# A retention-and-MLP kernel: the first product of the second-to-last chunk with seven products for eight, its sums by kind

## The chip, the core and the metric

One core of one Trainium2 chip. The metric is the device time of one execution in microseconds (us); a kernel's time is the median of its runs.

## The reference

Retention attention, then a two-layer perceptron with GELU. It is cut here to what is computed, for batch B = 4, heads H = 8, sequence S = 768, head size D = 64:

```python
for t in range(S):
    state = gamma * state + outer(k[t], v[t])      # for each batch and head
    y[t] = scale * q[t] @ state
x = y as (3072 tokens, 512)                        # d_model = 512
h = x @ w_in                                       # d_ff = 2048
out = gelu_tanh(h) @ w_out                         # back to 512
```

## The kernel before, in words

**Chunks and stages.** The sequence is cut into six chunks of 128 steps (c = 0 to 5, `NCk` = 6), each with the four batches, so 512 tokens. A chunk goes through three stages: attention, which leaves its tokens in `xT[c]`; M1, x times `w_in` with the GELU, which leaves g; and M2, g times `w_out`, which leaves the output rows. While PE works on M1 and M2 of chunk c, the attention of chunk n = c + 1 is put between their matmuls, and chunk m = c + 2 is loaded and prepared (`load`, `prep_qk`, `prep1`).

**What sets the order.** The order is written out by hand. `run(units, after)` goes through a list of units, and behind unit i it issues what `after[i]` lists. Each engine takes its own instructions strictly in the order in which the program issues them. In the loop `for c in range(2, NCk)` the 16 units 0 to 15 are M1 and the 14 units 16 to 29 are M2.

**M2 with seven products.** `units_w(c)` computes M2 of 2 x 2 blocks with seven products instead of eight. The table `PROD` lists them as n = 0 to 6: bank (X or Z), left operand, right operand. A block operand is a pair such as (0, 0); an operand that is a sum of blocks is a number, its kind 1 to 4. Each unit is one product n for one half a (eight matmuls, with fp = 0 to 7 in order), so unit 16 is n = 0, a = 0, unit 20 is n = 2, a = 0, and unit 26 is n = 5, a = 0. Product 2 uses the sum of kind 2, product 3 kind 1, product 4 kind 3, and product 5 kind 4. The sums of g are made by `g_sums(eng, c, f0, f1, p0, p1, keys)`: for each kind in `keys` one elementwise instruction of 128 x 512 on POOL or DVE (`tt`, line 387), for the pairs fp = f0 to f1 - 1. Kind 1 is the sum of g blocks (0, 1) and (1, 1), kind 2 is kind 1 minus block (0, 0), kind 3 is (0, 0) minus (0, 1), kind 4 is (1, 0) minus kind 2. `win_sums` and `x_sums` make the like sums of `w_in` and of x, on DVE.

**M1 in two forms.** In chunks 2 to 4, `moe1(c, fc)` computes M1 the plain way: each unit has four matmuls of 512 columns (line 348) and one GELU (line 364). In chunk 5, `units_h(c)` uses seven products: four groups G = 0 to 3, each with seven products of four matmuls with 256 columns (line 571). Its parts are `first` (products 0 and 1), `second` (2 and 3), `third` (4 and 5) and product 6. `keep` copies a bank to SBUF (product 0 on ACT, 2 on DVE, 3 on the engine named in the call), `add` adds such a copy to a bank, on DVE (products 1, 4, 5), and `many((G, n), ...)` issues GELUs on ACT. A product that goes on in a bank (n = 2, 4, 6 in X, n = 5 in Z) waits until the bank's copy or add has read it. The GELU of product 5 gives block (0, 0) of g, of product 4 block (1, 0), of product 1 block (0, 1), of product 6 block (1, 1). Group G covers the pairs fp = 2G and 2G + 1, so `g_sums(..., 4, 6, ...)` needs group 2 and `g_sums(..., 6, 8, ...)` group 3.

**Attention in pieces.** `att_AY(c, bs, tag, ca, abs_, eng)` computes the outputs of chunk c for the batches `bs` (`mm_yc`, `mm_yi`, then `ev_Y` on DVE into `xT`) and the scores of chunk `ca` for the batches `abs_` (`mm_A`, then `ev_A`, DVE's product with the mask into `a_sb`). `att_S` updates the state; for the last chunk there is nothing to update. Scores take two banks of the four with the tag "att"; `units_h` holds one such bank for each group from product 0 to the group's last GELU.

**Slots.** The load tiles q32 and k32 have 8 slots each and v32 has 6; `win_sums`, `x_sums` and the copies of `units_h` use free slots of these for their results.

Of the kernel before, what the change touches and what calls it, by code (L numbers as in the profile page):

```python
# [16 lines left out]
def kernel(  # L17
# [12 lines left out]
    NCk = S // C  # L30
# [3 lines left out]
    NF = d_ff // 128  # L34
# [25 lines left out]
    att = ctx.enter_context(tc.tile_pool(name="att", bufs=4))  # L60
# [79 lines left out]
    def copy_on(eng, out, in_):  # L140
        if eng is nc.scalar:
            eng.copy(out=out, in_=in_)  # L142
        else:
            eng.tensor_copy(out=out, in_=in_)
# [31 lines left out]
    def bank(tag, dt=F32, shape=(128, NHP, 128), name="ps"):  # L176
        return psum.tile(list(shape), dt, tag=tag, bufs=BANKS[tag], name=name)
# [167 lines left out]
    def moe1_mm(c, fc, out, t0, t1):  # L345
        wi, wr = w_in_of[fc]
        for kc in range(NHP):
            nc.tensor.matmul(  # L348
                out=out,
                lhsT=w_in_sb[wi][:, kc, wr * 128:(wr + 1) * 128],  # L350
                rhs=xT[c][:, kc, t0:t1],
                start=(kc == 0),
                stop=(kc == NHP - 1),
                skip_group_check=True,
            )

    def g_tile(c, fc):
        if (c, fc // 8) not in g_sb:
            g_sb[c, fc // 8] = gp.tile([128, 8, B * C], F16, tag=f"g{fc // 8}", name="g")
        r = fc % 8 // 2 * 2  # L360
        return g_sb[c, fc // 8][:, r:r + 2]

    def gelu(out, in_):
        nc.scalar.activation(out=out, in_=in_, func=AF.Gelu_apprx_tanh, scale=1.0)  # L364

    def moe1(c, fc):
        h_ps = bank("h", shape=(128, B * C), name="h_ps")
        moe1_mm(c, fc, h_ps, 0, B * C)
        gelu(g_tile(c, fc)[:, fc % 2], h_ps)
# [16 lines left out]
    def tt(eng, out, in0, in1, op):  # L386
        eng.tensor_tensor(out=out, in0=in0, in1=in1, op=op)  # L387
# [8 lines left out]
    def g_sums(eng, c, f0, f1, p0=0, p1=2, keys=(1, 2, 3, 4)):  # L396
        g = g_sb[c, f0 // 4].rearrange("p (f r) (a b t) -> p r b f a t", r=2, a=2, b=2)
        i = f0 % 4
        q = {
            (r, b): g[:, r, b][:, i:i + f1 - f0, p0:p1] for r in range(2) for b in range(2)  # L400
        }
        t = {j: s_g[j][:, f0:f1, p0:p1] for j in s_g}
        ops = (
            (1, q[0, 1], q[1, 1], ALU.add),
            (2, t[1], q[0, 0], ALU.subtract),
            (3, q[0, 0], q[0, 1], ALU.subtract),
            (4, q[1, 0], t[2], ALU.subtract),
        )
        for j, in0, in1, o in ops:
            if j in keys:  # L410
                tt(eng, t[j], in0, in1, o)
# [33 lines left out]
    def x_blk(c, K, col):  # L445
        x = xT[c].rearrange("p (K k) (a b t) -> p K b k a t", K=2, a=2, b=2)
        return x[:, K, 1 - col]
# [101 lines left out]
    def units_h(c):  # L549
        ps, snap = {}, {}  # L550

        def lhs_h(key, pr, k):
            if key in s_g:
                return t_in[key, pr // 4][:, k, pr % 4]
            K, r = key
            wi, wr = w_in_of[2 * pr + r]
            return w_in_sb[wi][:, 2 * K + k, wr * 128:(wr + 1) * 128]

        def rhs_h(key, k):
            if key in s_g:  # L560
                return s_x[c, (key - 1) // 2][:, (key - 1) % 2, k]
            return x_blk(c, *key)[:, k]

        def mm(G, n):
            k, lk, rk, new, stop = PROD[n]
            if new:
                tag = "att" if k == "X" else "h" if n == 1 else "o"
                ps[G, k] = bank(tag, shape=(128, 2, 2, 128), name="h_ps")
            for p in range(2):
                for kc in range(2):  # L570
                    nc.tensor.matmul(  # L571
                        out=ps[G, k][:, p],
                        lhsT=lhs_h(lk, 2 * G + p, kc),
                        rhs=rhs_h(rk, kc),
                        start=(new and p == 0 and kc == 0),
                        stop=(stop and kc == 1),
                        skip_group_check=True,
                    )

        def keep(eng, G, n):  # L580
            tag = {0: "q32", 2: "k32", 3: "v32"}[n]
            t = ld.tile([128, 2, 2, 128], F32, tag=tag, bufs=6 if n == 3 else 8, name="h_sb")
            copy_on(eng, t, ps[G, PROD[n][0]])
            snap[G, SNAP[n]] = t

        def add(G, n):
            t = snap[G, ADD[n][2]]
            tt(nc.vector, t, ps[G, PROD[n][0]], t, ALU.add)

        def act(G, n):  # L590
            r, col, nm = ADD.get(n, (1, 0, None))
            p0 = 2 * G
            if (c, p0 // 4) not in g_sb:
                g_sb[c, p0 // 4] = gp.tile([128, 8, B * C], F16, tag=f"g{p0 // 4}", name="g")
            g = g_sb[c, p0 // 4].rearrange("p (f r) (a b t) -> p r b f a t", r=2, a=2, b=2)
            gelu(
                g[:, r, 1 - col][:, p0 % 4:p0 % 4 + 2],
                snap[G, nm] if nm else ps[G, "X"],
            )

        V, A = nc.vector, nc.scalar

        def first(G):
            mm(G, 0)
            keep(A, G, 0)
            mm(G, 1)
            add(G, 1)

        def second(G, eng):
            mm(G, 2)  # L610
            keep(V, G, 2)
            mm(G, 3)
            keep(eng, G, 3)

        def third(G):
            mm(G, 4)
            add(G, 4)
            mm(G, 5)
            add(G, 5)

        def many(*what):
            for G, n in what:
                act(G, n)

        return [
            lambda: first(0),
            lambda: first(1),
            lambda: (second(0, A), many((0, 1))),
            lambda: (second(1, V), many((1, 1))),
            lambda: third(0),  # L630
            lambda: (third(1), many((0, 4), (0, 5))),
            lambda: (mm(0, 6), many((0, 6), (1, 4))),
            lambda: first(2),
            lambda: mm(1, 6),
            lambda: (first(3), many((1, 5), (1, 6))),
            lambda: (second(2, A), many((2, 1))),
            lambda: (second(3, V), many((3, 1))),
            lambda: third(2),
            lambda: (third(3), many((2, 4), (2, 5))),
            lambda: (mm(2, 6), many((2, 6), (3, 4))),  # L640
            lambda: (mm(3, 6), many((3, 5), (3, 6))),
        ]

    def units_0():
# [92 lines left out]
    def run(units, after):  # L737
        for i, u in enumerate(units):
            u()
            for f, *args in after.get(i, ()):  # L740
                f(*args)

    VE, AC, PO, SY = nc.vector, nc.scalar, nc.gpsimd, nc.sync
# [172 lines left out]

    for c in range(2, NCk):
        n, m = c + 1, c + 2
        after = {} if n == NCk else {
            12: [(att_AY, n, (), "att", n, (0, 1), None)],  # L920
            19: [(att_AY, n, (0, 1), "h", n, (2, 3), VE)],
            22: [(att_S, n, 0, 1)],
            25: [(att_AY, n, (2, 3), "h", n, (), AC), (att_S, n, 2, 3)],
        }

        def more(at, *what):
            after[at] = after.get(at, []) + list(what)

        for i in range(4 if n < NCk else 0):
            at = 4 * i + 3  # L930
            after[at] = [(g_sums, PO, c, 2 * i, 2 * i + 2)] + after.get(at, [])
        if n == NCk:
            t12, t34 = (1, 2), (3, 4)
            after = {
                7: [(g_sums, PO, c, 0, 2, 0, 2, t12)],
                9: [(g_sums, PO, c, 2, 4, 0, 2, t12), (g_sums, PO, c, 0, 2, 0, 2, t34)],
                15: [(g_sums, VE, c, 4, 6, 0, 2, t12), (g_sums, VE, c, 6, 8, 0, 2, t12)],
                19: [(g_sums, VE, c, i, i + 2, 0, 2, t34) for i in (2, 4, 6)],
            }
        if c in (3, 4):  # L940
            for i in range(2):
                more(i, (win_sums, 2 * (c - 3) + i))
        if c == 4:
            more(27, (x_sums, n))
        if m < NCk:
            more(0, (load, m))
            for b in range(B):
                more((18, 20, 23, 26)[b], (prep_qk, m, b))
                more(24, (prep1, PO, "v", m, b))
        m1 = units_h(c) if n == NCk else [(lambda fc=fc: moe1(c, fc)) for fc in range(NF)]  # L950
        run(m1 + units_w(c), after)


# [28 lines left out]
```

## Time and profile before

| | |
|---|---|
| median of 7 runs | 206.87 us (206.63 to 207.76) |
| profiled execution | 207.08 us |
| its span, first to last instruction | 205.3 us |
| busy: PE, DVE, ACT, POOL | 194.6, 119.6, 104.4, 128.8 us |
| M1 of chunk 4 (plain), on PE | 145.97 to 160.57 us |
| M2 of chunk 4, on PE | 160.57 to 175.70 us |
| M1 of chunk 5 (seven products), on PE | 175.70 to 189.05 us |
| sum of g on POOL, 128 x 512 | 1.153 us each |
| the same sum on DVE | 0.42 us (0.46 with kind 1) |
| GELU of 128 x 512 | 0.60 us from PSUM, 0.63 from SBUF |
| copy or add of a bank on DVE | 0.68 us |

Busy time is the union of an engine's instructions; the chain of waits goes back from the last instruction to what released it, step by step. In lines of the profile, L387 is a line of the kernel, `o_ps<-w_out,g` is output tile and input tiles, x16 a count, and brackets hold the idle time before an instruction and what ended it. PEld is PE's weight load. Times of a stage are taken at the start of PE's first matmul of it.

### The profile page before, as it was taken

To read this page: it belongs to the slowest core of one execution; us is meant where nothing else is said; L and a number is where in the kernel's file an instruction comes from. 1 tells how busy PE (TensorE), PEld (TensorE's weight loads), DVE (VectorE), ACT (ScalarE), POOL (GpSimd) and SP (SyncE) were. 2 spreads that over 40 slices of the span, in tenths; PEclk is the share of its full clock that TensorE was granted. 3 is DMA by queue.
4 is the path that set the end of the run, shared out by engine and by line. 5 is a ranking of instruction groups with operands and counts; after the bars stand their busy time and mean duration, and the time that the engine had idled before them with its cause. 6 is when DMAs were issued, how large, how long until landed. Compare 5 with 4: busy or idle time off the path is not lost.

```text
span 205.3 us, 4729 instructions
## 1 busy us (share of the span) xinstructions
PE 194.6 (95%) x1916; PEld 140.4 (68%) x1916; DVE 119.6 (58%) x271; ACT 104.4 (51%) x186; POOL 128.8 (63%) x130
## 2 busy tenths in 40 slices
PE   5697999999999999999999999999999999998993
PEld 1355746877688888644778644778644788886882
DVE  5256669669970449701379911289902284889730
ACT  2284464463379417566545365635365411588321
POOL 0589333952189999389997269997269980239000
PEclk9999999999999999999999999999999999999999
DMA  6999999999976797999995999842430000400004
GB/s 155 287 263 207 206 206 265 348 317 206 345 175 102 176 241 171 206 286 240 220 208 130 107 337 231 200 102 54 126 129 3 2 0 3 204 3 0 2 22 185
DMA packets 87094, 34.24 MB, mean 167 GB/s; under 512 B 80032, under 2 KB 84512, under 8 KB 87072
## 3 DMA queue, kind: packets, MB, share of 16 engines
q1 hardware_dynamic: 73920, 19.25, 44.3%
q0 software_dynamic: 6624, 12.58, 23.7%
q10 hardware_dynamic: 6528, 2.10, 4.1%
q8 instruction: 15, 0.25, 0.5%
q14 instruction: 7, 0.06, 0.1%
HBM read 27.63 MB, written 6.29 MB: 165 GB/s over the span
## 4 chain that ended last, share of the span: by engine, by line
PE 81%; ACT 5%; DVE 4%; DMA 3%; POOL 3%; SPq 2%; issue 1%; DVEq 0%; ACTq 0%
PE h_ps L348 33%; PE o_ps L490 30%; ACT g L364 4%; DMA k<-in_k_dram 3%; PE o_ps L654 3%; PE y_ps L242 3%; PE a_ps L207 3%; PE o_ps L687 2%; PE y_ps L229 2%; DVE st L285 2%; POOL qk L158 2%; PE s_ps L266 1%; PE h_ps L571 1%; SPq L85 1%; POOL w_in L329 1%; DVE h_sb L387 1%
## 5 line engine op out<-in xcount | busy, mean ns | idle before, releaser
L348 PE MATMUL h_ps<-xT,w_in 128*128 128x512 f16 (+2 forms) x424 | 73.6, 327 | 0.5 <-ACT g L364 0.5
L364 ACT ACTIVATE g<-h_ps 128x512 f16<-128x512 f32 (+1 forms) x86 | 50.3, 588 | 29.1 <-PE h_ps L348 28.9
L348 PEld LDWEIGHTS <-w_in 128*128 128x128 f16 x424 | 39.1, 98 | 30.2 <-issue 1.8
L220 DVE TENSOR_TENSOR a_sb<-a_ps,mask 128x512 f16<-128x512 f32 x48 | 30.1, 683 | 37.8 <-PE a_ps L207 37.7
L387 POOL TENSOR_TENSOR s_g<-g 128x512 f16<-128x512 f16 x35 | 40.3, 1153 | 15.9 <-ACT g L364 15.8
L490 PEld LDWEIGHTS <-s_g 128*128 128x128 f16 x320 | 30.2, 98 | 4.7 <-POOL s_g L387 0.7
L490 PE MATMUL o_ps<-t_w,s_g 128*128 128x256 f16 x240 | 28.1, 273 | 0.0
L490 PEld LDWEIGHTS <-g 128*128 128x128 f16 x240 | 23.4, 98 | 3.9 <-ACT g L364 0.6
L158 POOL TENSOR_TENSOR v<-v,cst 128x512 f16<-128x512 f32 x20 | 20.3, 1041 | 5.9 <-DMA v<-in_v_dram 5.8
L387 POOL TENSOR_TENSOR s_g<-s_g,g 128x512 f16<-128x512 f16 x18 | 20.8, 1153 | 1.4
L285 DVE SCALAR_TENSOR_TENSOR st<-st,cst,s_ps 64x128 f16<-64x128 f16 (+1 forms) x80 | 20.6, 318 | 0.7 <-PE s_ps L266 0.5
L387 POOL TENSOR_TENSOR s_g<-g,s_g 128x512 f16<-128x512 f16 x17 | 19.6, 1154 | 0.0
L490 PE MATMUL o_ps<-w_out,g 128*128 128x256 f16 x160 | 18.5, 273 | 0.3 <-ACT g L364 0.3
L523 POOL DMA_DIRECT2D out_dram<-o_sb x8 | 5.9, 737 | 16.2 <-DVE o_sb L387 15.3
L258 DVE TENSOR_TENSOR xT<-y_ps,dec 128x512 f16<-128x512 f32 x20 | 13.0, 686 | 4.0 <-PE y_ps L242 3.8
L142 ACT CAST qk<-q 128x512 f16<-128x512 f32 x20 | 12.4, 620 | 3.8 <-DMA q<-in_q_dram 3.7
L387 DVE TENSOR_TENSOR o_sb<-o_ps,s_p 128x512 f32<-128x512 f32 (+1 forms) x7 | 4.3, 616 | 15.8 <-ACT qk L142 8.0
L142 ACT CAST qk<-k 128x512 f16<-128x512 f32 x20 | 12.4, 621 | 0.6 <-DMA k<-in_k_dram 0.4
L519 ACT COPY o_sb<-o_ps 128x512 f32<-128x512 f32 (+1 forms) x5 | 2.7, 543 | 18.2 <-PE o_ps L490 17.6
L513 ACT COPY s_u<-o_ps 128x512 f32<-128x512 f32 (+1 forms) x6 | 3.1, 515 | 17.2 <-PE o_ps L490 12.0
L490 PE MATMUL o_ps<-w_out,s_g 128*128 128x256 f16 x80 | 9.6, 273 | 0.0
L490 PE MATMUL o_ps<-t_w,g 128*128 128x256 f16 x80 | 9.5, 273 | 0.0
(77 smaller groups left out, 230.2 us busy)
## 6 DMA issues: line engine op xcount, KB each, us to landing
out_dram<-o_sb POOLq DMA_DIRECT2D x10, 512.0 KB, 4.7
k<-in_k_dram SPq DMA_DIRECT2D x18, 256.0 KB, 4.7
q<-in_q_dram SPq DMA_DIRECT2D x18, 256.0 KB, 4.5
v<-in_v_dram SPq DMA_DIRECT2D x18, 256.0 KB, 5.2
w_in<-in_moe_w_in_dram POOLq DMA_DIRECT2D x4, 512.0 KB, 8.7
w_out<-in_moe_w_out_dram POOLq DMA_DIRECT2D x4, 512.0 KB, 13.8
q<-in_q_dram POOLq DMA_DIRECT2D x4, 256.0 KB, 11.2
k<-in_k_dram POOLq DMA_DIRECT2D x4, 256.0 KB, 9.5
```

The source lines that it names most:

```text
L142: eng.copy(out=out, in_=in_)
L158: eng.tensor_tensor(out=t, in0=src, in1=cst[:, col:col + H].unsqueeze(2).broadcast_to([128, H, Dh]), op=ALU.mult,)
L207: nc.tensor.matmul(out=ps[j][:, hp], lhsT=t[j * 64:(j + 1) * 64, 1, hp], rhs=t[j * 64:(j + 1) * 64, 0, hp], start=True, stop=True,)
L220: nc.vector.tensor_tensor(out=s, in0=ps[j], in1=mask[:, j], op=ALU.mult)
L242: nc.tensor.matmul(out=y_ps[j * 64:(j + 1) * 64, hp], lhsT=h16["v", c, b][:, 2 * hp + j], rhs=a_sb[c, b, j][:, hp], start=(c == 0), stop=True,
L258: nc.vector.tensor_tensor(out=x, in0=ps, in1=dec, op=ALU.mult)
L285: nc.vector.scalar_tensor_tensor(out=t[:, :, hp], in0=t[:, :, hp], scalar=cst[sl, OG + hp:OG + hp + 1], in1=s_ps[sl, :, hp], op0=ALU.mult, ...
L348: nc.tensor.matmul(out=out, lhsT=w_in_sb[wi][:, kc, wr * 128:(wr + 1) * 128], rhs=xT[c][:, kc, t0:t1], start=(kc == 0), stop=(kc == NHP - ...
L364: nc.scalar.activation(out=out, in_=in_, func=AF.Gelu_apprx_tanh, scale=1.0)
L387: eng.tensor_tensor(out=out, in0=in0, in1=in1, op=op)
L490: nc.tensor.matmul(out=po, lhsT=lhs(c, lk, fp, a), rhs=rhs(rk, fp), start=(new and fp == 0 and (last or a == 0)), stop=(stop and fp == NP ...
L654: nc.tensor.matmul(out=ps[k][:, a], lhsT=lhs(0, lk, fp, a), rhs=rhs(rk, fp), start=(first and fp == 0 and a == 0), stop=(stop and fp == NP ...
```

## The change

Five things are changed.

- M1 of chunk 4 is computed by `units_h` too (`seven = c >= NCk - 2`), with the sums it needs: `win_sums` runs in chunks 2 and 3 instead of 3 and 4, and `x_sums` for chunk 4 is issued behind unit 28 of chunk 3, for chunk 5 behind unit 28 of chunk 4 (it was 27).
- In chunk 4 the attention of chunk 5, which stood behind the units 12, 19 and 25, stands behind 17, 21 and 26, all in M2.
- In chunk 4 the sums of g, four kinds at a time behind the units 3, 7, 11 and 15 before, are ordered by kind: kinds 1 and 2 of group 0 behind unit 7, kinds 1 and 2 of group 1 and kind 3 of group 0 behind unit 9, and the other eleven behind unit 15. All are on POOL as before.
- In chunk 5 the sums behind unit 19 are ordered by kind as well (kind 3 of the groups 1 to 3, then kind 4).
- In `units_h`, which both chunks now use, the copy of product 3 in group 3 is made by ACT instead of DVE, and the last GELUs come in the order (3, 5), (3, 4), (2, 6), (3, 6) instead of (2, 6), (3, 4), (3, 5), (3, 6).

```diff
-            lambda: (second(3, V), many((3, 1))),
+            lambda: (second(3, A), many((3, 1))),
             lambda: third(2),
             lambda: (third(3), many((2, 4), (2, 5))),
-            lambda: (mm(2, 6), many((2, 6), (3, 4))),
-            lambda: (mm(3, 6), many((3, 5), (3, 6))),
+            lambda: (mm(2, 6), many((3, 5), (3, 4))),
+            lambda: (mm(3, 6), many((2, 6), (3, 6))),
...
     for c in range(2, NCk):
         n, m = c + 1, c + 2
+        seven = c >= NCk - 2
         after = {} if n == NCk else {
+            17: [(att_AY, n, (), "att", n, (0, 1), None)],
+            21: [(att_AY, n, (0, 1), "h", n, (2, 3), VE)],
+            26: [(att_AY, n, (2, 3), "h", n, (), AC)],
+        } if seven else {
             12: [(att_AY, n, (), "att", n, (0, 1), None)],
             19: [(att_AY, n, (0, 1), "h", n, (2, 3), VE)],
             22: [(att_S, n, 0, 1)],
...
-        for i in range(4 if n < NCk else 0):
-            at = 4 * i + 3
-            after[at] = [(g_sums, PO, c, 2 * i, 2 * i + 2)] + after.get(at, [])
-        if n == NCk:
-            t12, t34 = (1, 2), (3, 4)
-            after = {
-                7: [(g_sums, PO, c, 0, 2, 0, 2, t12)],
-                9: [(g_sums, PO, c, 2, 4, 0, 2, t12), (g_sums, PO, c, 0, 2, 0, 2, t34)],
-                15: [(g_sums, VE, c, 4, 6, 0, 2, t12), (g_sums, VE, c, 6, 8, 0, 2, t12)],
-                19: [(g_sums, VE, c, i, i + 2, 0, 2, t34) for i in (2, 4, 6)],
-            }
-        if c in (3, 4):
+        def sums(eng, keys, *fs):
+            for f in fs:
+                g_sums(eng, c, f, f + 2, 0, 2, keys)
+
+        if not seven:
+            for i in range(4):
+                after[4 * i + 3] = [(g_sums, PO, c, 2 * i, 2 * i + 2)] + after.get(4 * i + 3, [])
+        elif n < NCk:
+            more(7, (sums, PO, (1, 2), 0))
+            more(9, (sums, PO, (1, 2), 2), (sums, PO, (3,), 0))
+            more(15, (sums, PO, (1, 2), 4, 6), (sums, PO, (3,), 2, 4, 6), (sums, PO, (4,), 0, 2, 4, 6))
+        else:
+            more(7, (sums, PO, (1, 2), 0))
+            more(9, (sums, PO, (1, 2), 2), (sums, PO, (3, 4), 0))
+            more(15, (sums, VE, (1, 2), 4, 6))
+            more(19, (sums, VE, (3,), 2, 4, 6), (sums, VE, (4,), 2, 4, 6))
+        if c in (2, 3):
             for i in range(2):
-                more(i, (win_sums, 2 * (c - 3) + i))
-        if c == 4:
-            more(27, (x_sums, n))
+                more(i, (win_sums, 2 * (c - 2) + i))
+        if c >= NCk - 3 and n < NCk:
+            more(28, (x_sums, n))
...
-        m1 = units_h(c) if n == NCk else [(lambda fc=fc: moe1(c, fc)) for fc in range(NF)]
+        m1 = units_h(c) if seven else [(lambda fc=fc: moe1(c, fc)) for fc in range(NF)]
```

## The prediction

> **What bounds the kernel now.** I read the chain of waits first, then the stages, then the two stretches that the change touches, engine by engine. The chain gives TensorE (PE) 81% of the span. From 60 us on it is nearly unbroken PE work, up to the first matrix product (M1) of the last chunk. Stage lengths and busy times, cut where PE changes from M1 to M2 (start:end, length, then busy us of PE, weight load, DVE, ACT, POOL):
>
> ```profile
> 130.09:145.97 15.88, 15.88 (x210) 13.74 (x208) 11.07 (x27) 6.50 (x12) 11.95 (x12) 1.00 0.46 104
> 145.97:160.57 14.60, 14.60 (x83) 6.62 (x81) 5.69 (x13) 9.54 (x16) 11.52 (x11) 1.00 0.18 73
> 160.57:175.70 15.13, 15.13 (x177) 13.16 (x176) 7.87 (x14) 2.35 (x4) 8.49 (x9) 1.00 0.01 2
> 175.70:189.05 13.35, 12.74 (x115) 10.92 (x113) 11.54 (x20) 10.67 (x21) 6.95 (x8) 1.00 0.20 80
> ```
>
> These are M2 of chunk 3, M1 and M2 of chunk 4, M1 of chunk 5. Where all products are eight-fold (second row) PE is the only limit. Where seven products are used (last row), DVE and ACT are busy 11.5 and 10.7 of 13.35 us and PE starts to wait. The chain of waits says the same:
>
> ```profile
> 146.13 11.35 PE h_ps L348 x52
> 157.48 0.55 PE a_ps L207 x16
> 158.03 2.70 PE h_ps L348 x12
> 160.73 3.49 PE o_ps L490 x32
> ...
> 186.69 0.69 DVE h_sb L387
> 187.38 0.02 issue
> 187.40 2.76 ACT g L364 x5
> 190.16 0.05 issue
> 190.21 11.76 PE o_ps L490 x106
> ```
>
> The last five GELUs, behind DVE's adds, hold M2 of chunk 5. PE's timeline has both waits in brackets:
>
> ```profile
> 188.61 0.60 PE L571 MATMUL h_ps<-s_x,w_in 128*128 128x256 f16 x4 [0.60 <-DVE h_sb L387]
> 189.05 0.82 PE L490 MATMUL o_ps<-w_out,g 128*128 128x256 f16 x6
> 190.21 3.01 PE L490 MATMUL o_ps<-w_out,g 128*128 128x256 f16 x26 [0.34 <-ACT g L364]
> ```
>
> POOL, in chunk 4, makes 16 sums without a gap, from 150.37 on:
>
> ```profile
> 150.37 1.14 POOL L387 TENSOR_TENSOR s_g<-g 128x512 f16<-128x512 f16 x1 [2.28 <-ACT g L364]
> ...
> 165.28 1.15 POOL L387 TENSOR_TENSOR s_g<-s_g,g 128x512 f16<-128x512 f16 x1
> 166.40 1.15 POOL L387 TENSOR_TENSOR s_g<-g 128x512 f16<-128x512 f16 x1
> 167.51 1.15 POOL L387 TENSOR_TENSOR s_g<-g,s_g 128x512 f16<-128x512 f16 x1
> ```
>
> 16 sums from 150.37 to 168.66 are 1.143 us each. The one at 165.28 is the last sum of kind 2. It ends at 166.43, and product 2, which started at 165.72, reads it as its seventh operand (fp 6), at 165.72 + 6 x 0.109 = 166.38. So POOL's list is **already level with PE here**, and each operand is waited for alone.
>
> **What the Trainium skill says.** "TensorE: Matmul & The Clock Gate", Back-to-back issue gap: a warm matmul of N columns takes N/2.4 + 2.5 ns, 109 ns at 256; the chain has 32 in 3.49 us, 109. "ScalarE: Activation LUTs", What ACT_TABLE_LOAD costs: 186 ns + 0.833 N, back-to-back ones overlapping by 93, an estimated 520 ns at 512; the trace has GELUs 520 to 537 apart. "GPSIMD Engine Reference", Engine selection: a two-input elementwise operation is about 2x slower than on VectorE; here it is worse, 1.153 us against 0.42 for the same sum. "SBUF — State Buffer", on the shared port pair: a DVE operation with two SBUF inputs and a POOL operation exclude each other. This fits DVE's sum at 189.22, which took 0.92 while POOL worked until 189.86.
>
> **How I replay M1 with seven products.** Each engine works in program order. From the timelines: 4 matmuls 0.437 us, results 0.16 later; a DVE copy or add of PSUM 0.68 long, next start 0.60 later; a GELU 0.62, next 0.53 (from PSUM 0.58, 0.48); an ACT copy 0.585, next 0.47; 0.04 from engine to engine. Gn below is group G, product n. A product that accumulates waits for the copy or add of what its bank holds. The replay of chunk 5 before, against its trace, in us from the stage's start on PE, and of the stages after:
>
> | | trace 5 before | replay 5 before | replay 4 after | replay 5 after |
> |---|---|---|---|---|
> | first add (0,1) | 1.31 | 1.30 | 1.73 | 1.30 |
> | GELU (0,6) ends | 6.96 | 6.95 | 7.15 | 6.95 |
> | product (3,6) starts | 12.91 | 12.91 | 12.68 | 12.48 |
> | M1 ends on PE | 13.35 | 13.34 | 13.11 | 12.91 |
> | GELU (3,5) ends | 14.45 | 14.46 | 13.88 | 13.68 |
> | GELU (2,6) ends | 13.41 | 13.41 | 14.90 | 14.70 |
> | GELU (3,6) ends | 14.94 | 14.95 | 15.38 | 15.18 |
>
> In chunk 4 the first add is 0.43 later, because DVE makes x_sums(4) at 146.23 to 147.7 (the place and length of four of today's win sums); the end is 0.2 later for it.
>
> **Part by part.**
> *Copy (3,3) to ACT.* DVE loses 0.60, so add (3,4), for which product (3,6) waits, comes 0.43 sooner, bounded then by the earlier matmuls. ACT gains 0.47: copy (3,3) at 10.52, GELU (3,1) 10.99, (2,4) 11.52, (2,5) 12.06 (chunk 4).
> *GELU order.* (3,5) goes ahead but waits for add (3,5), which ends at 13.22, while ACT idles 0.6. Then (3,5) 13.26, (3,4) 13.79, (2,6) 14.32, (3,6) 14.80. M2's product 0 needs (3,5) at its seventh matmul and gets it sooner; but (2,6), which the sums of group 2 need, is **1.3 us later** than in the old order.
> *Chunk 5.* M2's seventh matmul starts at max(12.91 + 0.66, 13.68 + 0.06) = 13.74, where today it is at 190.21 - 175.70 = 14.51: **-0.77**. DVE's sums: (2,6) ends 14.70, the four of kinds 1, 2 are done by 16.7, and product 2 wants the last at 17.2; kinds 3, 4 are done by 19.7, product 4 starts at 20.1. Nothing new is late, so the 0.77 lasts to the end. If POOL's six sums (7.05 to 14.2) ran into DVE's, 0.5 would be lost of that.
> *Chunk 4, PE alone.* M1 falls from 14.60 (14.05 of products, 0.55 of attention scores) to 13.11, of which 112 x 0.109 = 12.2 is work. M2 is 15.13 + 0.55 (the scores moved in) plus 0.16 wait for GELU (3,5) and 0.13 for the score banks, which group 3's GELU frees: 15.97 in all, sum 29.0 against 29.73: -0.7.
> *POOL's list in chunk 4.* Still 16 sums, but five in M1 (7.24 to 13.15) and **eleven** (4 of kinds 1 and 2, 3 of kind 3, 4 of kind 4) behind GELU (2,6): 14.99 + 11 x 1.142 = 27.55. On the way the last of kind 2 ends at 19.56; product 2 would read it at 13.11 + 0.16 + 3.49 + 0.69 + 0.66 = 18.1, so PE waits 1.5. Then product 2 ends at 20.70, attention 1.66 to 22.36, product 3 to 24.11, product 4 (kind 3 done at 23.0) to 25.86; product 5 reads the last of kind 4 at 26.5 and gets it at 27.60: 1.1 more. After that come 2 matmuls 0.22, attention 1.11, and 24 matmuls 2.62: 31.55. So chunk 4 takes 31.55 for 29.73: **+1.82**.
> *Attention at 17, 21, 26.* The same instructions. DVE: masks of batches 2, 3 end at 26.1, unit 26 needs them at 27.8; x_sums(5) ends at 32.5, 0.95 into chunk 5, before the first add at 1.3. Cover 0.35; without it M1 of chunk 5 would slip by what exceeds it.
> *Win sums a chunk sooner.* In M1 of chunk 2 DVE has a gap of 10.96 before 96.89; eight sums take 3.0. Nothing. They hold four slots of the load tiles sooner; SP issues chunk 4's loads (88.55 on) behind the transposes of chunk 3, whose casts free the other four. Nothing; a load held past 103 us would delay the casts.
> *POOL's stores* of chunk 4 stand behind the sums but are ready only at about 31: nothing.
>
> **Sum.** +1.82 - 0.77 = +1.05. The profiled execution took 207.08 (span 205.3), within 0.1% of the median 206.87: 206.87 + 1.05 = **207.9**.
>
> **Unknown costs.** PE's waits of 1.5 and 1.1 us are longer than any in its steady part. The Trainium skill ("TensorE: Matmul & The Clock Gate", The HAM clock gate) puts the fall to half clock after some 3.4 us idle, which this trace doesn't show, so I take 0; one such window at half clock would cost an estimated 1.7. A sum on POOL could be 1.11 (its shorter spacing here) to 1.15 long: -0.4 to +0.1. The replay's error was 0.05; with x_sums in front, 0.3 either way.
>
> **Rivals.**
> 1. *Faster, POOL's list is not late.* Then -0.7 - 0.77: 205.4. It decides if the eleven sums end by 25.0, when product 5 would want the last without any wait: 0.91 us a sum, or GELU (2,6) 2.5 us sooner. For it: PE has less work in both chunks. Against: 35 sums of this form at 1153 ns.
> 2. *Chunk 5 gains nothing*, because ACT takes over what DVE sheds (M1 there already has ACT at 10.67 of 13.35): 206.87 + 1.8 = 208.7. Against: (3,5) needs only add (3,5).
> 3. *POOL's list is late, but less*: kind 2 overlaps more, or (2,6) comes 0.5 to 1 us sooner since ACT's small waits shrink: 207.1, no measurable difference.
>
> **Chances.** Forecast 0.62 (207.5 to 208.4), rival 2 and worse 0.12, rival 3 0.14, rival 1 0.12. About 0.3% (0.62 us) can be told from no change: slower 0.74, same 0.14, faster 0.12. The range goes from 206.9, inside rival 3, to 208.7.
>
> **What would show it.** Chunk 4: M1 some 13.1 on PE; waits of PE for s_g on POOL near 2.6 us in all, 0.7 today; POOL idle 1.8 before eleven sums in a row; the last of them some 4 us before chunk 5 starts. Chunk 5: M1 12.9, product (3,6) without most of its 0.60 wait. Wrong: POOL waits under 1 us, or GELU (2,6) before 14.0.

## The result, and the profile after

The kernel after takes 208.16 us (median of 15 runs, 207.66 to 209.29) against 206.96 us (36 runs) for the kernel before: ratio 1.0066, 95% interval 1.0050 to 1.0082. It is **slower by 1.0 to 1.7 us**; the prediction was 207.9, 0.9 to 1.0 above before.

The stages after, cut as before where PE changes from one product to the next (start:end, length, then busy us of PE, weight load, DVE, ACT, POOL): M1 and M2 of chunk 4, M1 of chunk 5, M2 of chunk 5 to the end.

```profile
145.69:158.87 13.18, 12.87 (x115) 10.93 (x113) 12.02 (x22) 10.62 (x20) 7.16 (x7) 1.00 0.20 81
158.87:177.27 18.40, 16.25 (x195) 13.34 (x193) 10.28 (x19) 3.77 (x7) 12.96 (x13) 1.00 0.00 1
177.27:190.33 13.06, 12.75 (x115) 10.93 (x113) 11.03 (x19) 10.64 (x20) 6.60 (x8) 1.00 0.21 82
190.33:206.30 15.97, 12.56 (x114) 10.77 (x111) 6.10 (x17) 4.89 (x12) 1.14 (x2) 0.99 0.18 67
```

M1 of chunk 4 is 1.42 shorter than its 14.60, and M2 of chunk 4 is 3.27 longer than its 15.13 (0.55 of each difference is the attention scores, which moved from M1 to M2). Together chunk 4 takes 31.58 for 29.73. PE works 16.25 of the 18.40 us of M2; what it waits for stands in its timeline:

```profile
163.25 0.82 PE L490 MATMUL o_ps<-t_w,s_g 128*128 128x256 f16 x6
165.51 1.26 PE L490 MATMUL o_ps<-t_w,s_g 128*128 128x256 f16 x10 [1.44 <-POOL s_g L387]
...
171.78 0.82 PE L490 MATMUL o_ps<-w_out,s_g 128*128 128x256 f16 x6
173.30 0.39 PE L490 MATMUL o_ps<-w_out,s_g 128*128 128x256 f16 x2 [0.70 <-POOL s_g L387]
```

Product 2 stops after six matmuls, and so does product 5: at fp = 6, where the sum of group 3 is read. The bracket is smaller than the time lost, since the modelled end of a matmul lies about 0.16 behind its issue: six matmuls of 0.109 from 163.25 end at 163.90, so 1.6 us are lost there, and from 171.78 in the same way 0.87. POOL's timeline gives the reason:

```profile
157.76 1.16 POOL L387 TENSOR_TENSOR s_g<-g 128x512 f16<-128x512 f16 x1
160.72 1.15 POOL L387 TENSOR_TENSOR s_g<-g 128x512 f16<-128x512 f16 x1 [1.81 <-ACT g L364]
161.95 1.16 POOL L387 TENSOR_TENSOR s_g<-s_g,g 128x512 f16<-128x512 f16 x1
163.07 1.16 POOL L387 TENSOR_TENSOR s_g<-g 128x512 f16<-128x512 f16 x1
164.31 1.15 POOL L387 TENSOR_TENSOR s_g<-s_g,g 128x512 f16<-128x512 f16 x1
165.41 3.38 POOL L387 TENSOR_TENSOR s_g<-g 128x512 f16<-128x512 f16 x3
168.75 4.49 POOL L387 TENSOR_TENSOR s_g<-g,s_g 128x512 f16<-128x512 f16 x4
```

POOL has nothing to do for 1.81 us, and then makes eleven sums in a row, from 160.72 to 173.24. The fourth ends at 165.46, and PE goes on at 165.51; the last ends at 173.24, and PE goes on at 173.30. The chain of waits now runs over POOL, and in chunk 5 no longer over the GELUs:

```profile
159.01 1.64 ACT g L364 x3
160.66 0.07 issue
160.72 1.16 POOL s_g L387
...
166.52 6.73 POOL s_g L387 x6
173.25 0.05 issue
173.30 0.39 PE o_ps L490 x2
...
189.89 0.60 PE h_ps L571 x4
190.49 0.66 PE o_ps L490 x6
191.15 0.01 issue
191.16 11.76 PE o_ps L490 x106
```

GELUs still matter in chunk 5, though the chain names none there: the load of weights for the seventh matmul of M2, the first that reads g of group 3, waits for one. It is GELU (3,5), which ACT begins at 190.47 and which takes 0.62:

```profile
191.15 2.73 PEld L490 LDWEIGHTS <-g 128*128 128x128 f16 x26 [0.29 <-ACT g L364]
```

The line with x106 is the rest of M2 of chunk 5 from its seventh matmul, 11.76 us in both kernels. It begins 13.89 us after chunk 5's start (191.16 - 177.27), where it was 14.51: 0.62 gained. The sum of the traces is +1.85 in chunk 4, -0.62 in chunk 5, and chunk 4 itself began 0.28 sooner in this execution: +0.95 in all, which the spans (206.3 and 205.3) show too.

### The profile page after: what moved, and what is told of

It reads as the page before. It is cut to its first block, busy times and chain, and to the rows that moved or that the text cites. A ratio compares the mean times of both kernels' runs of the same rounds, so it can differ in the third digit from the quotient of the medians.

```text
span 206.3 us, 4864 instructions
## 1 busy us (share of the span) xinstructions
PE 193.7 (94%) x1964; PEld 144.6 (70%) x1964; DVE 129.8 (63%) x291; ACT 107.0 (52%) x194; POOL 129.1 (63%) x130
## 4 chain that ended last, share of the span: by engine, by line
PE 78%; DMA 7%; POOL 6%; DVE 4%; ACT 2%; issue 1%; ACTq 1%; DVEq 0%; POOLq 0%
PE h_ps L348 26%; PE o_ps L490 26%; PE h_ps L571 12%; POOL s_g L387 6%; DMA w_in<-in_moe_w_in_dram 4%; PE o_ps L654 3%; DMA k<-in_k_dram 3%; PE y_ps L242 3%; PE a_ps L207 2%; PE o_ps L687 2%; PE y_ps L229 2%; DVE st L285 2%; ACT g L364 1%; PE s_ps L266 1%; DVE h_sb L387 1%
## 5 line engine op out<-in xcount | busy, mean ns | idle before, releaser
L348 PE MATMUL h_ps<-xT,w_in 128*128 128x512 f16 (+2 forms) x360 | 59.3, 318 | 0.6 <-ACT g L364 0.5
L364 ACT ACTIVATE g<-h_ps 128x512 f16<-128x512 f32 (+1 forms) x74 | 42.9, 586 | 24.1 <-PE h_ps L348 23.9
L348 PEld LDWEIGHTS <-w_in 128*128 128x128 f16 x360 | 32.9, 98 | 23.1 <-issue 1.5
L387 DVE TENSOR_TENSOR h_sb<-h_ps,h_sb 128x512 f32<-128x512 f32 x24 | 15.2, 684 | 3.2 <-ACT h_sb L142 2.8
L364 ACT ACTIVATE g<-h_sb 128x512 f16<-128x512 f32 x24 | 14.4, 633 | 2.9 <-DVE h_sb L387 2.9
L571 PEld LDWEIGHTS <-t_in 128*128 128x128 f16 x128 | 12.5, 98 | 2.3 <-issue 0.6
L571 PE MATMUL h_ps<-s_x,t_in 128*128 128x256 f16 x96 | 12.3, 272 | 0.0
```

The lines of the kernel that those rows point to most:

```text
L348: nc.tensor.matmul(out=out, lhsT=w_in_sb[wi][:, kc, wr * 128:(wr + 1) * 128], rhs=xT[c][:, kc, t0:t1], start=(kc == 0), stop=(kc == NHP - ...
L571: nc.tensor.matmul(out=ps[G, k][:, p], lhsT=lhs_h(lk, 2 * G + p, kc), rhs=rhs_h(rk, kc), start=(new and p == 0 and kc == 0), stop=(stop an ...
```

## The experiments

My theory was that of the prediction: POOL's eleven sums behind GELU (2,6) set the length of chunk 4. The main rival was that seven products and the moved attention cost by themselves, POOL only filling their waits; the second was that chunk 5's gain isn't real. The table has, for each kernel, the median with that of the kernel before on the same chip, the ratio to it with its 95% interval, and from the trace the length of chunk 4 on PE and the start of the seventh matmul of M2 in chunk 5, counted from chunk 5's start.

| kernel | us (before) | ratio | chunk 4 | seventh matmul |
|---|---|---|---|---|
| before | 206.96 | 1 | 29.73 | 14.51 |
| after | 208.16 (206.96) | 1.0066 (1.0050 to 1.0082) | 31.58 | 13.89 |
| chunk 5's share alone | 206.49 (206.84) | 0.9977 (0.9962 to 0.9993) | 29.75 | 13.93 |
| after, GELU (2,6) first | 206.56 (206.84) | 0.9977 (0.9963 to 0.9990) | 29.87 | 13.88 |
| after, one sum in the gap | 207.13 (206.84) | 1.0009 (0.9993 to 1.0025) | 30.69 | 13.88 |
| after, kinds 1, 2 on DVE | 207.76 (206.84) | 1.0033 (1.0019 to 1.0047) | 31.06 | 13.88 |
| after, sums not read | 205.86 (206.98) | 0.9953 (0.9936 to 0.9971) | 29.09 | 13.88 |
| (2,6) first, two sums on DVE | 206.07 (206.98) | 0.9950 (0.9936 to 0.9963) | 29.04 | 13.88 |
| (2,6) first, one sum on DVE | 205.76 (206.98) | 0.9942 (0.9927 to 0.9956) | 29.16 | 13.88 |
| chunk 5's share, (2,6) first | 206.50 (206.98) | 0.9974 (0.9959 to 0.9988) | 29.74 | 13.92 |
| before, copy on ACT | 206.54 (206.84) | 0.9979 (0.9964 to 0.9995) | 29.73 | 14.25 |
| before, order only | 206.56 (206.84) | 0.9989 (0.9973 to 1.0005) | 29.74 | 14.18 |

**What chunk 4 takes without waits for sums.** The edit, in `lhs`:

```diff
         if key in s_g:
+            if c == 4:
+                return g_sb[c, fp // 4][:, 2 * (fp % 4), 2 * a * C:(2 * a + 1) * C]
             return s_g[key][:, fp, a]
```

> The kernel after, but in M2 of chunk 4 the products that would read a sum of g read block (0, 0) of g in its place; POOL still makes all 16 sums, and nothing waits for them. It leaves out the use of the sums in chunk 4. It measures what chunk 4 takes on PE, ACT and DVE alone. My theory: no wait for POOL is left, chunk 4 takes 29.0 to 29.3 for 31.6 us, 2.3 to 2.5 us faster than the kernel after, about 205.7. Rival (seven products and the moved attention cost by themselves): 207.5 or more.

Chunk 4 took 29.09: PE has the same matmuls, POOL makes the same sums, and 2.49 us are gone. This is the two stops of the kernel after (1.6 and 0.87). Product 2 and the first half of product 5 now run through (line numbers are two higher in this kernel):

```profile
165.16 1.91 PE L492 MATMUL o_ps<-t_w,g 128*128 128x256 f16 x16
172.08 1.04 PE L492 MATMUL o_ps<-w_out,g 128*128 128x256 f16 x8
```

The rival that the seven products cost by themselves falls: without the sums' waits the change is faster than the kernel before, ratio 0.9953 (0.9936 to 0.9971).

**GELU (2,6) sooner.**

```diff
-            lambda: (mm(2, 6), many((3, 5), (3, 4))),
-            lambda: (mm(3, 6), many((2, 6), (3, 6))),
+            lambda: (mm(2, 6), many((2, 6), (3, 5))),
+            lambda: (mm(3, 6), many((3, 4), (3, 6))),
```

> The kernel after, with the last four GELUs in the order (2,6), (3,5), (3,4), (3,6): (2,6) falls into the 0.57 us in which ACT waits for add (3,5), so (3,5) is not later. My theory (POOL's eleven sums behind GELU (2,6) set the length of chunk 4): POOL begins them 1.6 us sooner, at some 13.4 for 15.0 us into chunk 4, and chunk 4 takes 30.0 for 31.6: 1.6 us faster than the kernel after, about 206.6. Rival (the longer chunk 4 comes from M1 with seven products and the moved attention themselves, POOL only fills their waits): within 0.3 of the kernel after, 208.2.

Chunk 4 took 29.87, 1.71 less. ACT's timeline shows (2,6) at 159.21, and (3,5) no later than in the kernel after, 13.31 us into chunk 4 (159.86 - 146.55) for 13.32:

```profile
157.61 1.69 ACT L364 ACTIVATE g<-h_sb 128x512 f16<-128x512 f32 x3
159.21 0.58 ACT L364 ACTIVATE g<-h_ps 128x512 f16<-128x512 f32 x1
159.86 1.15 ACT L364 ACTIVATE g<-h_sb 128x512 f16<-128x512 f32 x2
```

POOL's eleven sums are then the end of a list without a gap (the x2 is the last sum of M1 and the first of the eleven), and PE keeps one wait only:

```profile
158.62 2.40 POOL L387 TENSOR_TENSOR s_g<-g 128x512 f16<-128x512 f16 x2
161.10 1.15 POOL L387 TENSOR_TENSOR s_g<-s_g,g 128x512 f16<-128x512 f16 x1
```

```profile
172.45 0.39 PE L490 MATMUL o_ps<-w_out,s_g 128*128 128x256 f16 x2 [0.66 <-POOL s_g L387]
```

Chunk 5 has its seventh matmul at 13.88, as in the kernel after. So the order of the change cost 1.7 us in chunk 4 and gained nothing over this one: (2,6) could have gone into ACT's 0.57 of waiting.

**One sum in POOL's gap.**

```diff
-            more(9, (sums, PO, (1, 2), 2), (sums, PO, (3,), 0))
-            more(15, (sums, PO, (1, 2), 4, 6), (sums, PO, (3,), 2, 4, 6), (sums, PO, (4,), 0, 2, 4, 6))
+            more(9, (sums, PO, (1, 2), 2), (sums, PO, (3,), 0, 2))
+            more(15, (sums, PO, (1, 2), 4, 6), (sums, PO, (3,), 4, 6), (sums, PO, (4,), 0, 2, 4, 6))
```

> The kernel after, with one sum of chunk 4 (kind 3 of group 1) moved ahead into POOL's idle 1.8 us before GELU (2,6) ends: ten sums behind it for eleven. My theory: kind 2 is as late as before (PE waits 1.4 in product 2), the last of kind 4 comes 1.14 sooner, so PE's second wait of 0.7 goes nearly whole, and what remains is the 1.4: 1.0 to 1.1 us sooner by the chain of sums, but no more than PE's second wait shows; 0.7 to 1.1 us faster than the kernel after, 207.1 to 207.5. Rival (POOL not deciding): 208.2.

Chunk 4 took 30.69, 0.89 less. The wait of PE in product 2 stayed (1.43 in its timeline, 1.44 in the kernel after) and that in product 5 went:

```profile
165.28 1.27 PE L490 MATMUL o_ps<-t_w,s_g 128*128 128x256 f16 x10 [1.43 <-POOL s_g L387]
...
171.55 1.04 PE L490 MATMUL o_ps<-w_out,s_g 128*128 128x256 f16 x8
```

POOL's gap shrank from 1.81 to 0.68. The expectation holds, and with it the reading that each kind has its own due time: one sum off the list helps only what is read behind it.

**Kinds 1 and 2 of groups 2 and 3 on DVE.**

```diff
-            more(15, (sums, PO, (1, 2), 4, 6), (sums, PO, (3,), 2, 4, 6), (sums, PO, (4,), 0, 2, 4, 6))
+            more(15, (sums, VE, (1, 2), 4, 6), (sums, PO, (3,), 2, 4, 6), (sums, PO, (4,), 0, 2, 4, 6))
```

> The kernel after, with the four sums of kinds 1 and 2 of groups 2 and 3 in chunk 4 on DVE for POOL; POOL keeps seven behind unit 15 and can begin them at 13.2 us without GELU (2,6). My theory if DVE and POOL run side by side: all sums are in time, chunk 4 takes 29.0 to 29.2, 2.4 us faster than the kernel after, about 205.7. Rival (a sum on DVE and one on POOL exclude each other, so each of DVE's four waits up to 1.14 us for POOL's, and the masks of the attention stand behind them): the last of kind 2 at up to 21.2, PE waits up to 3.1 us in product 2, chunk 4 up to 32.1, 208 to 208.7.

Chunk 4 took 31.06: the first expectation was wrong by 2 us. The rival had the direction right and the size too large (up to 32.1, and 208 us or more for 207.76). DVE's timeline:

```profile
161.06 0.76 DVE L387 TENSOR_TENSOR s_g<-g 128x512 f16<-128x512 f16 x1 [1.70 <-ACT g L364]
161.86 1.25 DVE L387 TENSOR_TENSOR s_g<-s_g,g 128x512 f16<-128x512 f16 x1
163.04 1.37 DVE L387 TENSOR_TENSOR s_g<-g 128x512 f16<-128x512 f16 x1
164.44 1.26 DVE L387 TENSOR_TENSOR s_g<-s_g,g 128x512 f16<-128x512 f16 x1
165.62 2.47 DVE L220 TENSOR_TENSOR a_sb<-a_ps,mask 128x512 f16<-128x512 f32 x4
```

The second to fourth sums take 1.25 to 1.37 where a sum alone takes 0.42. POOL's sums beside them are longer too (four in 5.03 for 4.49). The page "SBUF — State Buffer" of the Trainium skill, section "Who interferes with whom", says that a DVE instruction with two SBUF inputs and a POOL instruction that reads SBUF contend for a shared pair of ports, which one of them holds while the other waits. The trace agrees in that both get longer. DVE thus goes at POOL's pace while POOL is busy: the last of kind 2 ends at 165.70, 19.62 us into chunk 4, where POOL alone had it at 19.77 (165.46 - 145.69). Product 2 stops again (1.30 in the bracket, on DVE now), with a stop of 0.29 for the masks behind.

**Two sums, or one, of kind 4 on DVE.** With GELU (2,6) first, as above, and:

```diff
-            more(15, (sums, PO, (1, 2), 4, 6), (sums, PO, (3,), 2, 4, 6), (sums, PO, (4,), 0, 2, 4, 6))
+            more(15, (sums, PO, (1, 2), 4, 6), (sums, PO, (3,), 2, 4, 6), (sums, PO, (4,), 0, 2))
+            more(19, (sums, VE, (4,), 4, 6))
```

> The kernel after with the last GELUs in the order (2,6), (3,5), (3,4), (3,6), and with the sums of kind 4 of groups 2 and 3 in chunk 4 on DVE, behind unit 19, where DVE has some 4 us without work. POOL keeps nine sums in a row. My theory: DVE's two sums wait up to 1.1 us each for POOL's and hold POOL by some 0.4 each, both end by 22 us, POOL ends at 24.6, and PE's wait of 0.66 in product 5 goes: 0.6 to 0.7 faster than with the order alone (206.56), about 205.9, and faster than both kernels. Rival (the exclusion costs POOL and the attention behind DVE as much as it saves): 206.5 or more.

The second kernel leaves `(sums, PO, (4,), 0, 2, 4)` on POOL and has `(sums, VE, (4,), 6)`.

> As the kernel with two sums on DVE, but with only the sum of kind 4 of group 3 there. POOL keeps ten. My theory: POOL's last (kind 4 of group 2) ends at some 25.3, where PE wants it at 24.9: a wait of 0.3 to 0.5 is left of 0.66, so 0.2 to 0.4 faster than with the order alone, 206.2 to 206.4, between that and the kernel with two. Rival (exclusion): 206.6 or more.

Chunk 4 took 29.04 with two and 29.16 with one, against 29.87 with the order alone; with two, PE waits for no sum, and the length is that of the kernel in which the sums aren't read (29.09). The gain, 0.83, is a little more than the 0.6 to 0.7 expected, which was the bracket of 0.66 without the 0.16 that it leaves out. Both engines are held up here too, DVE's two sums taking 2.10 and POOL's three beside them 3.75 for 3.38, but nobody waits for it: DVE's next instruction starts 0.46 behind the first of the matmuls that it waits for (168.13, 167.67), as in the kernel after (168.16, 167.70).

```profile
165.95 2.10 DVE L387 TENSOR_TENSOR s_g<-g,s_g 128x512 f16<-128x512 f16 x2
```

```profile
165.33 3.75 POOL L387 TENSOR_TENSOR s_g<-g 128x512 f16<-128x512 f16 x3
```

Of the second kernel I expected a wait of 0.3 to 0.5 left, and it is nearly gone (0.12 of length), so the gain was larger than expected. Both kernels are faster than the kernel before, and so than the kernel after: 0.9950 (0.9936 to 0.9963) and 0.9942 (0.9927 to 0.9956). Which of the two is better, these intervals don't tell.

**What the seven products of chunk 4 are worth.** Chunk 4 plain, chunk 5 with its share of the change and (2,6) first:

> The kernel before with chunk 5's share of the change and the order (2,6), (3,5), (3,4), (3,6); chunk 4 stays plain. It tells what seven products in chunk 4 are worth once their sums are nearly in time. My theory: as with chunk 5's share alone, 0.4 to 0.7 us below the kernel before, 206.2 to 206.5, since (3,5) and (3,4) come at the same times; so the kernel with two sums on DVE should be 0.4 to 0.6 below this one. Rival (the seven products of chunk 4 give nothing even then): equal.

206.50 against 206.07 and 205.76 with seven products in chunk 4 on the same chip, 0.43 and 0.74 less; by the traces 29.74 for 29.04 and 29.16. Once their sums are in time, the seven products, with the attention moved as they need it, give 0.6 to 0.7 us.

**Chunk 5's share, whole and in its two parts.** Three kernels from the kernel before: the edits of `units_h` and the sums by kind in chunk 5; only `second(3, A)` for `second(3, V)`; only the order of the change.

> The kernel before with only chunk 5's share of the change: the copy of product 3 in group 3 on ACT, the new order of the last GELUs, the sums of kinds 3 and 4 by kind. Chunk 4 stays plain. My theory (the traces give chunk 5 0.62 us, the prediction 0.77): 0.6 to 0.8 us faster than the kernel before, about 206.3, the seventh matmul of M2 some 13.8 us after the start of chunk 5. Rival 2 (ACT takes over what DVE sheds): no difference, 206.9 to 207.0.

> The kernel before with one edit: the copy of product 3 in group 3 on ACT for DVE; the GELUs keep their order, chunk 4 stays plain. My theory (the replay): the seventh matmul of M2 in chunk 5 comes 14.1 us after the chunk's start for 14.5, 0.4 faster, about 206.5. Rival 2 (ACT becomes the limit in place of DVE): 14.5, no difference.

> The kernel before with one edit: the new order of the last GELUs, (3,5), (3,4), (2,6), (3,6); the copy stays on DVE, chunk 4 stays plain. My theory (the replay): GELU (3,5) starts when its add is ready, the seventh matmul at 14.2 for 14.5 us, 0.3 faster, about 206.6; the two edits add up to the 0.6 seen together. Rival (the order only moves ACT's wait): no difference.

By the traces the seventh matmul comes at 13.93, 14.25 and 14.18 for 14.51: 0.58 together, 0.26 from the copy, 0.33 from the order, so the parts add up, and nothing is left for the sums by kind. With the copy alone the chain of waits ends in ACT, with the order alone in DVE's adds, for which product (3,6) still waits 0.60:

```profile
186.53 3.27 ACT g L364 x6
189.80 0.05 issue
189.84 11.76 PE o_ps L490 x106
```

```profile
188.90 0.60 PE L571 MATMUL h_ps<-s_x,w_in 128*128 128x256 f16 x4 [0.60 <-DVE h_sb L387]
```

The times of the first two are below 1 by their intervals; that of the order alone (0.9989, 0.9973 to 1.0005) is not, so its 0.33 rests on the trace, and so does the adding up: by the ratios the whole share (0.1 to 0.8 us) can't be told from the copy alone (0.1 to 0.7). Rival 2, that chunk 5 gains nothing, is refuted. In part it holds: with the copy alone ACT's GELUs are the limit, and the copy gives 0.26 where 0.4 was expected.

## Why the prediction was right

*POOL's list in chunk 4*, the step on which the sign hung, held. GELU (2,6) was to end at 14.90 and POOL's eleven sums to run from 14.99 to 27.55; the trace has the sums from 15.03 (160.72 - 145.69) to 27.55 (173.24 - 145.69). That the end fits to 0.01 is luck in part: the first four sums took 4.74 (160.72 to 165.46) where four at 1.142 are 4.57, and the other seven 7.83 (165.41 to 173.24) where seven are 7.99. So PE, which was to stop for 1.5 and 1.1, stopped for 1.6 and 0.87. Chunk 4 was to take 31.55 and took 31.58. The prediction's 0.7 us of waits of PE for POOL's sums in the kernel before is not in that trace: from 140 us on PEld waits 0.2 us for them, and PE has no such wait in its timeline. That these stops are POOL's doing is shown by the kernel that doesn't read the sums (-2.49) and by the earlier GELU (-1.71).

*Chunk 4, PE alone*: 29.0 predicted, 29.09 measured. The prediction's own terms, 13.11 and 15.97, add up to 29.08.

*M1 with seven products*: 13.11 predicted for chunk 4, 13.18 measured; the replay, made from the trace of chunk 5, held for chunk 4.

*Chunk 5*: -0.77 predicted, -0.62 measured. This term was mis-sized, by 0.15. The prediction's rule for it was right: the seventh matmul starts 0.06 behind GELU (3,5), which was to end at 13.68 and ended at 13.82 (190.47 + 0.62 - 177.27); with 0.06 that is 13.88, and 13.89 was measured. (3,5) was late because the adds on DVE were. They begin at 10.68 (187.95 - 177.27), where the replay's 12.48 for product (3,6) needs 10.56 (less two spacings of 0.60, one add of 0.68 and 0.04), and DVE has a wait for PE's product before them. Of these 0.12, 0.05 is PE, which is that much later than in the trace before (product 5 of group 2 at 10.41 for 10.36), and the rest is about the step from the end of PE's product to DVE, 0.10 (187.85 to 187.95) where the replay had 0.04. Product (3,6) starts at 12.62 (189.89 - 177.27) for 12.48 and waits 0.30, half of the 0.60 before, where most of it was to go. The copy gave 0.26 where the replay had 0.43.

*GELU order*: (2,6) was said to come 1.3 us later than in the old order, which was not run in chunk 4 with seven products. Against the order with (2,6) first it ends 1.7 later (160.65 - 145.69 = 14.96 for 159.79 - 146.55 = 13.24). The order of the change was thus not the only one that has (3,5) early. I took it as given and did not see the better one.

*Unknown costs*: the cost of PE's longer waits for its clock was taken as 0; the clock granted to PE is 1.00 in M2 of chunk 4, as the table of stages shows, and chunk 5 behind it has the same length up to the seventh matmul (13.89) as in the kernel with two sums on DVE, where PE doesn't wait in chunk 4 for a sum (13.88).

*Win sums, loads, stores*, costed at nothing: chunks 2 and 3 take 30.47 and 30.48 us, as before (30.47 and 30.49), and chunk 5 shows no new wait for them. x_sums for chunk 5 ended at 177.87, 0.60 into chunk 5, sooner than the 0.95 of the replay.

The total, +1.05 predicted, is +1.2 by the medians and +1.0 to +1.7 by the ratio; by the traces' two stages it is +1.23.

## What to carry to other kernels

When a matmul-saving scheme adds sums on a slow engine, write the sums' due times beside their ready times: the last sums here were bound by when their input appears (one GELU) plus a list of eleven at 1.14 us, and not by the engine's total load, which was the same 16 sums. Reordering a producer's instructions for its first reader can push back a second reader that is the critical one; look for an order that uses the producer's own idle time. Moving sums from POOL to DVE paid here only where DVE could afford to run at POOL's pace.

## What the runs showed of the hardware that I had not expected

Beside POOL's list DVE's sums took 0.76 to 1.37 us for 0.42 alone, so one can wait for nearly a whole sum of POOL. POOL loses less, about 0.18 us for each sum of DVE: its three sums took 3.38 alone, 3.56 beside one sum on DVE and 3.75 beside two. That is less than the 0.42 of a sum on DVE, so the two do not simply take turns for their full lengths. What they share and for how long, these runs don't show.

Kernels that are the same up to chunk 4 differ by more ahead of it than in the stage behind it. In the seven kernels that have chunk 4 with seven products, chunk 4 began between 145.47 and 147.60 us, while the seventh matmul of chunk 5 came at 13.88 or 13.89 in each. For a change of half a microsecond the length of a stage in one trace tells more than the difference of two executions.
